# Where ScalarE pads keys and queries, and where VectorE finishes a choice, in a gated-attention and mixture-of-experts kernel

## The chip, the cores and the metric

The kernel runs on one core of a Trainium2 chip. The metric is the device time of one execution in microseconds (us). The engines are named as in the profile: PE is TensorE (PEld its weight loads), DVE is VectorE, ACT is ScalarE, POOL is GpSimd, and SP is the engine that issues most DMAs.

## The reference

```python
def _attn_ref(q, k, v, f_logit):              # all (4, 8, 768, 48)
    f = 1.0 / (1.0 + np.exp(-f_logit))
    for t in range(S):
        state = f[:, :, t, :, None] * state + np.einsum('bhd,bhe->bhde', k[:, :, t], v[:, :, t])
        y[:, :, t] = np.einsum('bhd,bhde->bhe', q[:, :, t], state)
    return y

def _moe_ref(x, w_gate, w1, w2, capacity):    # x (3072, 384), 8 experts, inner width 1024
    logits = x @ w_gate
    expert_idx = np.argmax(logits, axis=1)    # one expert per row, the first of equal ones
    ...                                       # its probability is gate_w
    disp[e, counts[e]] = x[i]                 # rows sorted by expert, up to the capacity
    ...
    h = np.maximum(np.einsum('ecd,edf->ecf', disp, w1), 0.0)
    y = np.einsum('ecf,efd->ecd', h, w2)
    out[i] = gate_w[i] * y[expert_idx[i], pos[i]]
```

The rows `x` of the second part are the attention outputs, all heads of a token side by side.

## The kernel before, in words

The attention half works in 24 chunks of 128 tokens (6 chunks for each of 4 batches), with all 8 heads of a chunk at once. It is written as a loop over slots n = 0 to 24. Each slot works at several chunks: in slot n the keys and queries of chunk n + 3 are padded, those of chunk n + 2 are transposed and scaled, scores of chunk n + 1 are made, the values of chunk n are applied, and the rows of chunk n - 1 are finished. Within this part the order of instructions on every engine is the order in which the code is written; nothing reorders it. The mixture of experts follows and is ordered by a scheduler.

The steps that matter here, with their lines:

- `kq_pad` (L407 on POOL in slots 0 to 6, L409 on ACT from slot 7, `PAD_ACT = 7`): copies a loaded chunk of keys and queries (`ld_kq`, 3 buffers) into a padded tile `kqp` (2 buffers), which `kq_in` of the next slot reads. Behind it `load("kq", n + 6)` issues the two DMAs (L210) that fill the buffer just read.
- `kq_in`: 16 PE transposes (L366) into two `psT` tiles in PSUM, which DVE scales into `kT` and `qT` (L415).
- `keys_pe` / `keys_out`: 8 PE transposes of the keys (L451) into the same `psT` pool of two, copied out by ACT as `kn` (L457).
- `scores_pe` / `scores_out`: 16 products (L426) into two `psA` tiles, copied out by ACT as `AT` (L432), then masked by POOL (L434).
- `update` (L488), then `rank_pe` (L675, L676, L679, L682), `rows_pe` (L543) and `values` (L522) follow on PE in that order. `update` and `rank_pe` write one `psA` tile, the side bank; `rows_pe` writes another; the pool has two.
- `y_out` (L534, `yT`), `rows_copy` (L559, `rows`) and `rows_parts` (L569, `parts`) on ACT. `rows` and `parts` read what `rows_pe` made and free that `psA` tile.
- `sig` (L357, `pf`) in even slots and `split_high` (L135) in slots 9, 11, 17, 20 to 23 stand on ACT as well.
- A choice of experts is made for a group of 3 or 4 chunks: `choose_sum` on POOL, `choose_max` on DVE (L583 to L586) at the end of a slot, and in the next slot `choose_first` (L591 `r_wm`, L593 `tally`) on DVE. This way is used for five groups, so that `choose_first` runs in slots 6, 10, 14, 17 and 20. In the same slot `rank_pe` on PE reads the choice: L675 and L676 read older tiles, L679 and L682 read the new `tally`.

The lines that make the ranking wait for the choice:

```python
    nc.tensor.matmul(pr, onesb, ohc.unsqueeze(1)..., start=(base is None), stop=False)      # L676
    for c in range(nch - 1):
        nc.tensor.matmul(pr[:, c + 1 :], onesb, oh[:, c].unsqueeze(1)..., ...)              # L679
    marks["rank"] = nc.tensor.matmul(pr, tri, oh, start=False, stop=True)                   # L682
```

Of the kernel before, what the change touches and what calls it, by code (L numbers as in the profile page):

```python
# [29 lines left out]
def kernel(  # L30
# [47 lines left out]
    PAD_ACT = 7  # L78
# [116 lines left out]
    def pairs(nm, n, nt):  # L195
        b, t0 = n // CPB, n % CPB * C
        return srcs[nm][b, :, t0 : t0 + nt, :].rearrange("h (t j) d -> t h (j d)", j=2)

    def load(nm, n):
        if n >= (NT // 2 if nm == "f" else NT):  # L200
            return
        t = loads[nm, n % NLOAD[nm]]
        if nm == "v":
            b, t0 = n // CPB, n % CPB * C
            nc.sync.dma_start(t[:, :, :D], srcs[nm][b, :, t0 : t0 + C, :].rearrange("h p d -> p h d"))
            return
        t = t.rearrange("t h j d -> t h (j d)")
        if nm == "kq":
            for h, x in enumerate(nm):
                nc.sync.dma_start(t[64 * h : 64 * h + 64], pairs(x, n, C))  # L210
        elif n == 0:
            for h, queue in enumerate((nc.sync, nc.scalar)):
                hs = slice(4 * h, 4 * h + 4)
                queue.dma_start(t[:64, hs], pairs(nm, 0, C)[:, hs])
        else:
            nc.sync.dma_start(t, pairs(nm, 2 * n, 2 * C))

    def loaded(nm, n):
        return loads[nm, n % NLOAD[nm]]
# [132 lines left out]
    def sig(u):  # L352
        if u >= NT // 2:
            return
        cuts = (0, 64, P) if u == 0 else (0, P)
        for r0, r1 in zip(cuts, cuts[1:]):
            pace["ins"] = nc.scalar.activation(  # L357
                pf[u % 2][r0:r1, :, :, :D], loaded("f", u)[r0:r1].rearrange("t h j d -> t j h d"), AF.Sigmoid
            ).ins
# [43 lines left out]
    def kq_pad(n):  # L403
        if n < NT:
            src = loaded("kq", n).rearrange("t h j d -> t j h d")
            if n - 3 < PAD_ACT:
                nc.gpsimd.tensor_copy(kqp[n % 2][:, :, :, :D], src)  # L407
            else:
                nc.scalar.activation(kqp[n % 2][:, :, :, :D], src, AF.Copy)  # L409

    def kq_in(n):
        pts = transposes(*((psT.tile([P, NP, C], F32, name="psT"), kqp[n % 2], h) for h in range(2)))
        for nm, pt, by, made in (("kT", pts[0], Sufb[n % 2], kTs), ("qT", pts[1], Rqs.pop(n), qTs)):
            t = abuf.tile([P, NP, C], F32, name=nm, bufs=3)
            nc.vector.tensor_tensor(t[:R].rearrange("r p t -> r (p t)"), pt, by[:R], op=ALU.mult)  # L415
            made[n] = t
# [22 lines left out]
    def first(n):  # L439
        return n % CPB == 0  # L440

    def last(n):
        return n % CPB == CPB - 1
# [145 lines left out]
    def choose_first(g, m, w):  # L589
        wm = abuf.tile([P, m], F32, name="r_wm")  # L590
        nc.vector.tensor_reduce(out=wm, in_=w, axis=AX.X, op=ALU.max)  # L591
        oh = tallies[-1][:, 1 : m + 1]
        nc.vector.tensor_tensor(oh, w, wm.unsqueeze(2).broadcast_to([P, m, NE]), op=ALU.is_equal)  # L593
        chosen[g] = oh, m
# [149 lines left out]
    def early_job(n, at):  # L744
        for step, arg in EARLY.get((n, at), ()):
            step(arg)
# [19 lines left out]
    quarters, half = [0] * DT, []  # L766
# [59 lines left out]
    def slot(n):  # L826
        slot_now["n"] = n
        prev, cur, nxt = 0 <= n - 1 < NT, 0 <= n < NT, 0 <= n + 1 < NT
        kqn, fn = 0 <= n + 2 < NT, 0 <= n + 3 < NT
        tail = n - 1 >= NT - NCH  # L830
        keyed = cur and not last(n)
        done = ends.get(n - 1)
        if keyed and n:
            keys_out(n, keys_pe(n))
        if prev and not (cur and first(n)):
            y_out(n - 1)
        if nxt:
            pas = scores_pe(n + 1)
        if 0 < n < PAD_ACT:
            kq_pad(n + 3)  # L840
        if n == 3:
            nc.gpsimd.tensor_copy(ring[:, :, DM + NE : W], tokid[:, :RING].unsqueeze(2))
        while half:
            choose_first(*half.pop())
        for g in full:
            choose_sum(*g)
        if n == 1:
            f_in(4)
        if kqn:
            kq_in(n + 2)  # L850
        if n % 2 and fn and n not in (1, 9, 15):
            f_in(n + 3, n + 4)
        if nxt:
            scores_out(n + 1, pas)
        if n == 0:
            sig(2)
        if prev and cur and first(n):
            y_out(n - 1)
        if n % 2 == 0 and n > 0 and fn:
            sig((n + 4) // 2)  # L860
        if n in PIECE_SPLIT:
            split_high(pieces[PIECE_SPLIT.index(n)])
        loads_of(n)
        early_job(n, 0)
        if cur:
            inter(n)
        if n in (9, 15):
            f_in(n + 3, n + 4)
        early_job(n, 1)
        if keyed:  # L870
            pu = update(n)
        if split_at["n"] == n:
            pc = split_pe()
        ranks = [(g, chosen[g][1], rank(g, None)) for g in list(chosen) if not done or g != done[0]]
        if keyed:
            state(n, pu)
        if split_at["n"] == n:
            split_count(pc)
        ranked = [(g, m, pick(*job)) for g, m, job in ranks]
        if tail:  # L880
            for g, m, job in ranked:
                put(*job)
                queue.extend(range(g, g + m))
            ranked = []
        if keyed:
            carry(n)
        if n == 0:
            kq_pad(3)
            load("kq", 6)
        if nxt:  # L890
            for s in range(SCATTERS.get(n, 2)):
                flush_scatter()
        if fn:
            F = decay(n + 3)
        if prev:
            px = rows_pe(n - 1)
            if tail:
                rows_logits(n - 1, px)
                rows_copy(n - 1, px)
                chosen[n - 1] = choose_one(row_at(n - 1), abuf, tallies[-1][:, 1:2]), 1  # L900
            else:
                rows_copy(n - 1, px)
                rows_parts(n - 1, px)
        if fn and n >= PAD_ACT:
            kq_pad(n + 3)
            load("kq", n + 6)
        if n in QUARTERS:
            k, parts = QUARTERS[n]
            for part in range(parts):
                split_low(pieces[k], nc.gpsimd, PARTS, quarters[k])  # L910
                quarters[k] += 1
        if fn:
            decay_back(n + 3, F)
        for g, m, job in ranked:
            put(*job)
            queue.extend(range(g, g + m))
            if g + m == SPLIT:
                split_at["n"] = n + 1
        while full:
            g = full.pop()  # L920
            half.append((*g, choose_max(*g)))
        if prev and done and not tail:
            g, m = done
            if n - 1 >= NT - 2 * NCH:
                sum_parts(g, m)
                chosen[g] = choose(rows_at(g, m), m, abuf, tallies[-1][:, 1 : m + 1]), m
            else:
                full.append(done)
        if cur:
            values(n)  # L930
        if n % 2 == 0 and n and fn:
            load("f", (n + 4) // 2 + 2)
        if n == 1:
            f_in(5)
        if tail:
            early_job(n, 2)
            g, m = done
            place(*rank(g, psT))
            queue.extend(range(g, g + m))
            flush_scatter()  # L940
        else:
            early_job(n, 2)
        for k in pieces:
            if k >= DT and PIECE_SPLIT[k] == n:
                split_low(pieces[k], nc.vector)
        if n == 4:
            nc.gpsimd.tensor_copy(cap, cap_i[:, 0:1])
        if n == NT - 5:
            ins = nc.sync.dma_start(xg0, dispv[0, : T_FIRST[0]].rearrange("(k p) w -> p k w", p=P))
            tc.declare_no_dep(ins.ins, group="late", reason="later tokens of this expert go to rows of their own")  # L950
            after(ins, early_ins[0], "the rows of the early tokens")
        if n == NT - 3:
            checks.append(check_decay())
        if n == NT - 2:
            pc = psT.tile([P, 1], F32, name="psT")
            nc.tensor.matmul(pc, onesb[:R], checks[0][:R], start=True, stop=True)
            nc.vector.tensor_copy(bad_i, pc)
# [533 lines left out]
```

## Time and profile before

| what | value |
|---|---|
| median of 3 runs | 373.35 us (372.59, 373.35, 375.57) |
| the profiled execution's own time | 375.17 us |
| its span, first to last instruction | 373.4 us |
| PE busy | 362.1 us, 97% of the span |
| DVE busy | 247.8 us, 66% |
| ACT busy | 223.8 us, 60% |
| POOL busy | 166.5 us, 45% |
| slots 7 to 20 (53.4 to 125.4 us of the span) | 72.0 us |
| mean granted clock of TensorE | 0.990 of full speed |

The profile is one execution, seen from its first to its last instruction; 1.8 us of its own time lie outside the span. A busy PE is one that has matmuls under way, not one at its peak. A time in the trace counts from the start of the span, and a number in brackets behind a row is the idle time of that engine before it, with what ended it.

### The profile page before, as it was taken

Reading aid. Unit: us, or ns where it says so; the run is one execution under the profiler, and the core shown is the slowest. Engines: PE = TensorE matmul, PEld = TensorE weight load, DVE = VectorE, ACT = ScalarE, POOL = GpSimd, SP = SyncE. Lnnn points to the kernel's source line nnn. Section 1 sums busy time; section 2 is a strip of 40 time slices with the busy share of each in tenths; the row PEclk is TensorE's granted clock in tenths of the full one; section 3 lists DMA queues with packets and bytes.
Section 4 is the critical chain, followed back from the end, with each engine's and each line's share of the span. In section 5 each row is a group of like instructions: output and inputs, shape, how many; then the busy total and the mean of one; then the engine's idle time right before and its main releaser. Section 6 shows DMA issues by size and latency. Waiting matters only on the chain.

```text
span 373.4 us, 10082 instructions
## 1 busy us (share of the span) xinstructions
PE 362.1 (97%) x3895; PEld 340.8 (91%) x3895; DVE 247.8 (66%) x533; ACT 223.8 (60%) x458; POOL 166.5 (45%) x275
## 2 busy tenths in 40 slices
PE   8999999999899999999999999999999999999993
PEld 7999898888787889999899999999999999999993
DVE  4898988979687866753676296857757665570300
ACT  3356677877586763255477475759578586583310
POOL 6665556675757675235613702127117244144012
PEclk9999999999899999999999999999999999999997
DMA  8999999999997432476696979799797997721001
GB/s 153 187 177 224 205 207 227 256 214 226 213 227 164 130 114 105 133 237 204 191 239 188 286 196 242 212 187 319 169 204 247 172 208 253 129 94 52 14 23 40
DMA packets 111351, 67.86 MB, mean 182 GB/s; under 512 B 93646, under 2 KB 105844, under 8 KB 111296
## 3 DMA queue, kind: packets, MB, share of 16 engines
q1 hardware_dynamic: 107504, 57.09, 69.1%
q0 software_dynamic: 3520, 9.97, 7.7%
q8 instruction: 32, 0.52, 0.6%
q14 instruction: 23, 0.19, 0.2%
q10 hardware_dynamic: 272, 0.10, 0.1%
HBM read 49.46 MB, written 11.43 MB: 163 GB/s over the span
## 4 chain that ended last, share of the span: by engine, by line
PE 84%; issue 8%; ACT 3%; POOL 2%; DVE 1%; POOLq 1%; ACTq 0%
PE psM L1222 15%; PE psA L754 9%; PE psM L1015 9%; PE psT L754 9%; PE psM L754 7%; PE psA L426 6%; PE psY L522 6%; PE psA L543 5%; PE psT L366 4%; PE psY L468 3%; PE psA L488 3%; PE psT L451 3%; PE psF L366 2%; POOL out_dram L326 2%; PE psA L376 2%
## 5 line engine op out<-in xcount | busy, mean ns | idle before, releaser
L326 POOL DMA_INDIRECT out_dram<-yo,g_ti x30 | 31.3, 1042 | 55.6 <-ACT yo L1019 31.7
L434 POOL TENSOR_SCALAR_AFFINE_SELECT AT<-AT 128x512 f32<-128x512 f32 x48 | 29.4, 637 | 23.3 <-ACT AT L432 23.2
L1015 PE MATMUL psM<-w2h,hh 128*128 128x384 f32 (+2 forms) x112 | 37.5, 340 | 0.0
L1015 PE MATMUL psM<-w2l,hh 128*128 128x384 f32 (+2 forms) x112 | 37.3, 338 | 0.0
L1015 PE MATMUL psM<-w2h,hl 128*128 128x384 f32 (+2 forms) x112 | 37.2, 338 | 0.0
L135 ACT ACTIVATE w2h<-raw 128x768 fp32r<-128x768 f32 x32 | 27.0, 844 | 11.2 <-DMA raw<-in_moe_w_dram 11.2
L1222 PE MATMUL psM<-hh,w2h 128*128 128x440 f32 (+3 forms) x96 | 33.7, 351 | 0.0
L1222 PE MATMUL psM<-hh,w2l 128*128 128x440 f32 (+3 forms) x96 | 33.7, 351 | 0.0
L1222 PE MATMUL psM<-hl,w2h 128*128 128x440 f32 (+3 forms) x96 | 33.6, 350 | 0.0
L144 DVE TENSOR_TENSOR w2l<-raw,w2h 128x768 fp32r<-128x768 f32 x28 | 27.8, 994 | 7.7 <-ACT w2h L135 6.9
L386 DVE TENSOR_TENSOR_SCAN Suf<-psF,direv 112x511 f32<-112x511 f32 x24 | 29.1, 1212 | 4.5 <-PE psF L366 4.5
L432 ACT ACTIVATE AT<-psA 128x512 f32<-128x512 f32 x48 | 26.4, 612 | 8.9 <-PE psA L426 5.6
L1242 POOL COPY yo<-yq 128x384 uint16<-128x384 uint16 (+4 forms) x16 | 11.9, 790 | 40.1 <-DMA yq<-yp 38.2
L426 PE MATMUL psA<-qT,kT 48*128 48x128 f32 x384 | 29.4, 293 | 0.0
L400 DVE TENSOR_TENSOR_SCAN Rq<-psF,d 112x512 f32<-112x512 f32 x24 | 29.4, 1223 | 0.0
L326 POOL DMA_INDIRECT disp<-rows,ri x24 | 24.8, 1034 | 9.5 <-issue 4.3
L144 DVE TENSOR_TENSOR w1l<-raw,w1h 128x1024 fp32r<-128x1024 f32 x21 | 26.5, 1269 | 2.9 <-ACT w1h L135 2.6
L761 DVE SCALAR_TENSOR_TENSOR hl<-psA,hh 128x224 fp32r<-128x224 f32 (+8 forms) x26 | 14.2, 547 | 21.3 <-ACT hh L760 19.3
L559 ACT ACTIVATE rows<-psA 128x384 f32<-128x384 f32 x24 | 11.8, 491 | 26.0 <-PE psA L543 19.6
L522 PE MATMUL psY<-AT,ld_v 128*48 128x128 f32 (+1 forms) x384 | 26.9, 278 | 0.0
L426 PEld LDWEIGHTS psA<-qT,kT 48*128 48x128 f32 x384 | 25.8, 201 | 0.5 <-issue 0.5
L135 ACT ACTIVATE w1h<-raw 128x1024 fp32r<-128x1024 f32 x24 | 24.8, 1060 | 1.9 <-DMA raw<-in_moe_w_dram 1.9
(253 smaller groups left out, 1041.7 us busy)
## 6 DMA issues: line engine op xcount, KB each, us to landing
raw<-in_moe_w_dram SPq DMA_DIRECT2D x24, 512.0 KB
raw<-in_moe_w_dram SPq DMA_DIRECT2D x32, 384.0 KB
ld_kq<-in_k_dram SPq DMA_DIRECT2D x24, 192.0 KB
ld_kq<-in_q_dram SPq DMA_DIRECT2D x24, 192.0 KB
ld_v<-in_v_dram SPq DMA_DIRECT2D x24, 192.0 KB
ld_f<-in_f_logit_dram SPq DMA_DIRECT2D x11, 384.0 KB
xg<-disp SPq DMA_DIRECT2D x6, 589.5 KB
xg<-disp SPq DMA_DIRECT2D x3, 393.0 KB
```

What stands on the lines that cost most here:

```text
L135: return nc.scalar.activation(hi, raw, AF.Copy)
L144: engine.tensor_tensor(lo[cs], raw[cs], hi[cs].bitcast(F32), op=ALU.subtract)
L326: ins = nc.gpsimd.indirect_dma_start(out=dst, out_offset=bass.IndirectOffsetOnAxis(ap=idx, axis=0), in_=rows, in_offset=None, bounds_check ...
L386: nc.vector.tensor_tensor_scan(out=_view(Suf[:R], m - 1, [[-1, m]]), data0=_view(F, m, [[-1, m]]), data1=_view(direv[:R], m - 1, [[-1, m]] ...
L400: nc.vector.tensor_tensor_scan(out=Rq[:R], data0=F, data1=d1[:R], initial=0.0, op0=ALU.mult, op1=ALU.max)
L426: nc.tensor.matmul(pas[s][:, p], kTs[n][r, p], qTs[n][r, p], start=True, stop=True)
L432: nc.scalar.activation(AT[:, s], pas[s], AF.Copy)
L434: nc.gpsimd.affine_select(AT[:, s], AT[:, s], pattern=[[0, NP], [1, C]], compare_op=ALU.is_ge, fill=0.0, base=0, channel_multiplier=-1)
L522: nc.tensor.matmul(py[b][64 * g : 64 * g + m, a, :], vt[:, 2 * p + s, :m], AT[:, s, p, :], start=(first(n) and a == 0), stop=(a == NP // 2 ...
L754: nc.tensor.matmul(ph[:, :T], a[:, c, fs], x[:, c, :T], start=(n == 0), stop=(n == 3 * DT - 1))
L1015: nc.tensor.matmul(py[:n], x[:, ks], a[:, ft], start=(ft == 0 and m == 0), stop=(ft == FT - 1 and m == 2))
L1222: nc.tensor.matmul(pys[c][:, :T], a[:, ft, cs], x[:, :T], start=(ft == 0 and n == 0), stop=(ft == FT - 1 and n == 2))
```

## The change

Two steps of `slot` are moved, and nothing is added or removed. `kq_pad(n + 3)` with its loads, for slots 7 to 20, moves from behind `rows_copy` and `rows_parts` to a place ahead of `split_high`, of the slot's other loads and of the row copies. `choose_first` moves from ahead of `kq_in(n + 2)` to behind it.

```diff
@@ -840,14 +840,14 @@
-        while half:
-            choose_first(*half.pop())
         for g in full:
             choose_sum(*g)
         if n == 1:
             f_in(4)
         if kqn:
             kq_in(n + 2)
+        while half:
+            choose_first(*half.pop())
         if n % 2 and fn and n not in (1, 9, 15):
             f_in(n + 3, n + 4)
@@ -858,6 +858,9 @@
         if n % 2 == 0 and n > 0 and fn:
             sig((n + 4) // 2)
+        if fn and n >= PAD_ACT:
+            kq_pad(n + 3)
+            load("kq", n + 6)
         if n in PIECE_SPLIT:
             split_high(pieces[PIECE_SPLIT.index(n)])
         loads_of(n)
@@ -901,9 +904,6 @@
                 rows_copy(n - 1, px)
                 rows_parts(n - 1, px)
-        if fn and n >= PAD_ACT:
-            kq_pad(n + 3)
-            load("kq", n + 6)
         if n in QUARTERS:
```

On DVE, in a slot with a choice (here the second of the five, slot 10), the two scalings `kT` and `qT` stood behind `r_wm` and `tally`; `-` is before, `+` is after.

```order
 L585 TENSOR_TENSOR r_w<-rows,r_m 128x32
 L586 TENSOR_TENSOR r_w<-r_w,desc 128x32
+L415 TENSOR_TENSOR kT<-psT,Suf_141 112x512
+L415 TENSOR_TENSOR qT<-psT,Rq 112x512
 L591 TENSOR_REDUCE r_wm<-r_w 128x4
 L593 TENSOR_TENSOR tally<-r_w,r_wm 128x32
-L415 TENSOR_TENSOR kT<-psT,Suf_141 112x512
-L415 TENSOR_TENSOR qT<-psT,Rq 112x512
 L502 TENSOR_TENSOR U<-psA,S_147 112x192
 L642 TENSOR_TENSOR r_sel<-psA,tally 128x4x8
```

The choice now stands between the scalings and `U`; PE's rows are the same in both kernels, L679 with its wait for DVE behind L488, L675 and L676.

On ACT, at the first of the fourteen moved pads (slot 7, which pads chunk 10):

```order
 L534 ACTIVATE yT<-psY 112x2x128 x2
 L432 ACTIVATE AT<-psA 128x512 x2
-L559 ACTIVATE rows<-psA 128x384
-L569 ACTIVATE parts<-psA 128x32
 L409 ACTIVATE kqp_122<-ld_kq_104 128x16x48
+L559 ACTIVATE rows<-psA 128x384
+L569 ACTIVATE parts<-psA 128x32
 L457 ACTIVATE kn<-psT 128x4x64
 L457 ACTIVATE kn<-psT 128x4x48
```

The pad stood between `parts` and the next slot's `kn`, and stands now between `AT` and `rows`.

On SP, the loads of the same two slots (7 and 8). Before:

```order
L205 DMA ld_v_114<-in_v_dram 128x8x48
L210 DMA ld_kq_104<-in_k_dram 64x8x96
L210 DMA ld_kq_104<-in_q_dram 64x8x96
L205 DMA ld_v_116<-in_v_dram 128x8x48
L122 DMA raw<-in_moe_w_dram 128x1024
L210 DMA ld_kq_105<-in_k_dram 64x8x96
L210 DMA ld_kq_105<-in_q_dram 64x8x96
```

After:

```order
L210 DMA ld_kq_104<-in_k_dram 64x8x96
L210 DMA ld_kq_104<-in_q_dram 64x8x96
L205 DMA ld_v_114<-in_v_dram 128x8x48
L210 DMA ld_kq_105<-in_k_dram 64x8x96
L210 DMA ld_kq_105<-in_q_dram 64x8x96
L205 DMA ld_v_116<-in_v_dram 128x8x48
L122 DMA raw<-in_moe_w_dram 128x1024
```

The loads of keys and queries go out ahead of the slot's values and of the expert weights (`raw`).

## Rows read from the trace of the kernel before

**Rows 1.** The page, part 1: busy us (share of the span) xinstructions.

```profile
PE 362.1 (97%) x3895; PEld 340.8 (91%) x3895; DVE 247.8 (66%) x533; ACT 223.8 (60%) x458; POOL 166.5 (45%) x275
```

**Rows 2.** Busy time by stretch: us, busy by engine (instructions), granted clock, DMA share, GB/s.

```profile
53.40:125.40 72.00, 68.89 (x1416) 60.23 (x1414) 60.00 (x128) 53.08 (x127) 46.90 (x79) 0.98 1.03 215
...
150.00:332.00 182.00, 182.00 (x1007) 176.30 (x1006) 119.39 (x245) 118.36 (x209) 62.96 (x66) 1.00 0.80 208
```

**Rows 3.** Waits of PE from 53.4 to 125.4: total us, times, longest.

```profile
PE psY L468 <- issue: 1.0, 2, 0.7
PE psA L488 <- ACT AT L432: 0.7, 3, 0.3
PE psT L366 <- ACT kn L457: 0.6, 3, 0.2
PE psT L366 <- issue: 0.6, 1, 0.6
```

**Rows 4.** Timeline of slot 10 (a choice): start us, us, engine, line [idle before].

```profile
66.22 0.18 DVE L591 TENSOR_REDUCE r_wm<-r_w 128x4 f32<-128x32 f32 x1
...
66.44 0.19 DVE L593 TENSOR_TENSOR tally<-r_w,r_wm 128x32 bf16<-128x32 f32 x1
...
66.57 0.69 DVE L415 TENSOR_TENSOR kT<-psT,Suf 112x512 f32<-112x512 f32 x1
...
67.18 0.68 DVE L415 TENSOR_TENSOR qT<-psT,Rq 112x512 f32<-112x512 f32 x1
...
67.77 0.22 PE L679 MATMUL psA<-tally,onesb 128*128 128x24 bf16 x3
...
68.13 0.36 DVE L502 TENSOR_TENSOR U<-psA,S 112x192 f32<-112x192 f32 x1 [0.27 <-PE psA L682]
```

**Rows 5.** Timeline of slots 6 and 17, two more choices.

```profile
46.65 0.68 DVE L415 TENSOR_TENSOR qT<-psT,Rq 112x512 f32<-112x512 f32 x1
...
46.96 0.22 PE L679 MATMUL psA<-tally,onesb 128*128 128x24 bf16 x3
...
105.79 0.68 DVE L415 TENSOR_TENSOR qT<-psT,Rq 112x512 f32<-112x512 f32 x1
...
106.19 0.19 PE L679 MATMUL psA<-tally,onesb 128*128 128x16 bf16 x2
```

**Rows 6.** The pad: its group in the list by line, then timelines around it.

```profile
L409 ACT ACTIVATE kqp<-ld_kq 128x768 f32<-128x768 f32 x14 | 11.9, 847 | 0.0
...
29.98 0.46 PE L451 MATMUL psT<-ident,kT 64*128 64x64 f32 x8
...
30.54 0.60 ACT L457 ACTIVATE kn<-psT 128x256 f32<-128x256 f32 x2 [0.73 <-PE psT L451]
...
74.92 1.79 SPq L210 DMA_DIRECT2D ld_kq<-in_q_dram  x1
...
77.17 0.87 ACT L357 ACTIVATE pf<-ld_f 128x768 f32<-128x768 f32 x1
...
78.16 0.49 ACT L559 ACTIVATE rows<-psA 128x384 f32<-128x384 f32 x1
...
79.20 1.12 PE L426 MATMUL psA<-qT,kT 48*128 48x128 f32 x16
...
83.54 0.49 ACT L559 ACTIVATE rows<-psA 128x384 f32<-128x384 f32 x1 [1.61 <-PE psA L543]
...
84.01 0.85 ACT L409 ACTIVATE kqp<-ld_kq 128x768 f32<-128x768 f32 x1
...
84.30 0.46 PE L451 MATMUL psT<-ident,kT 64*128 64x64 f32 x8
...
85.48 0.61 ACT L457 ACTIVATE kn<-psT 128x256 f32<-128x256 f32 x2 [0.63 <-PE psT L451]
```

**Rows 7.** Busy time by stretch, columns as in rows 2, around the lower clock.

```profile
99.00:100.00 1.00, 0.60 (x13) 0.43 (x12) 0.36 (x1) 0.63 (x1) 1.00 (x3) 0.96 1.20 288
100.00:101.00 1.00, 1.00 (x22) 1.00 (x20) 0.25 (x1) 0.00 (x0) 0.30 (x1) 0.50 1.15 263
```

## The prediction

> **What bounds the kernel now.** I read the page's first part, then the stretch that the change touches, then what PE waits for there. PE is busy for 97% of the span; no other engine passes 66% [rows 1]. The moved steps lie in slots 6 to 20. From 53.4 to 125.4 us PE is busy for 68.89 of 72.00 us, and from 150 to 332 us, in the mixture of experts, for all 182 [rows 2]. So a microsecond that PE gains or loses in the slots arrives at the end: nothing behind them has room to absorb it. The reader is to take two limits from this. No edit here can give back more than the 3.1 us that PE is idle in the stretch, and most of these do not hang on the moved steps: 1.6 us are "issue", 0.7 us wait for `AT` and 0.6 us for `kn` [rows 3]. A wait newly put in front of PE costs its full length.
>
> **The choice behind the scalings.** This half moves two short DVE instructions in five slots. In slot 10, `r_wm` starts at 66.22, `tally` 0.22 us later and lasts 0.19 us, so the choice is known at 66.63. PE's L679, which reads it, starts at 67.77 without waiting: the choice is 1.14 us early [rows 4]. What it delays is `kT`, which starts at 66.57. But `kT` cannot start before PE's transposes are out, and in four of the five slots DVE had nothing to wait for but those, or came free at the same moment; nobody waits for `kT` and `qT` before the next slot, since scores are made one slot after the scaling. So the gain from earlier scalings is zero, and what hides their cost today is a whole slot of distance.
>
> After the change the choice begins when `qT` lets DVE go. From `kT` to `qT` it takes 0.61 us from start to start [rows 4], so I let `r_wm` start 0.61 us behind `qT`, `tally` 0.22 us behind that, and end after 0.19 us (0.18 us where the group has three chunks): 1.02 us behind the start of `qT`. That start itself stays, because PE sets it.
>
> - Slot 10: 67.18 + 1.02 = 68.20, against L679 at 67.77: 0.43 us late.
> - Slot 6, the first chunk of a batch, has no L468 in PE's row, so L679 comes sooner: 46.65 + 1.02 = 47.67 against 46.96: 0.71 us [rows 5].
> - Slot 17, the last chunk of a batch, has no `update`: 105.79 + 1.01 = 106.80 against 106.19: 0.61 us [rows 5].
> - Slots 14 and 20 repeat slot 10 within 0.02 us: 0.43 us each.
>
> The sum is 2.6 us. A hand-over from one engine to the next comes on top. The trace has none from DVE to L679, since that matmul never waited. The nearest row is `kn` at 30.54, 0.10 us after the L451 it waited for was out at 29.98 + 0.46 [rows 6]; five of these make 0.5 us. That gives 2.6 to 3.1 us, and I take 2.9, nearer the upper end because every wait in these slots shows some hand-over. Queued behind L679 on PE are L682, L543 and L522, and behind the choice on DVE are `U`, which waits for L682 in any case [rows 4], and the two scans of the slot. So PE and DVE slip by about the same amount, `rows` on ACT slips with L543, and the next slot begins that much later. I see nothing that gives the time back.
>
> **The pads ahead of the row copies.** This half moves fourteen ACT instructions of 847 ns, which today never wait (idle before them 0.0 us in all) [rows 6]. Ahead of `rows` ACT is often idle, because `rows` waits for L543: 1.61 us in slot 13 [rows 6]. There the pad fits in without moving `rows`. Where `pf` stands in front and the slot is short, it does not: in slot 12 `pf` ends at 78.04 and `rows` starts at 78.16. A pad between them starts at about 77.95, 0.1 us of overlap as between the neighbours here, so `rows` starts 0.75 us after that, at about 78.7, and with its 0.49 and the 0.19 us of `parts`, less the overlaps, the `psA` tile is free at about 79.3. The scores that take it start at 79.20 and use the second tile with their second matmul: 0.1 us late. Slot 18 is the same case; the other twelve have idle time in front of `rows`, or the scores come late enough. I set the cost at 0.1 to 0.2 us.
>
> What could be gained is at the pad's old place, in front of `kn`. Without a pad, in slot 3, `kn` starts 0.56 us after L451 (29.98 to 30.54). With a pad it is often the same, but in six slots it is late; in slot 14 it starts at 85.48, 1.18 us after L451 and 0.63 us after the pad has ended [rows 6]. ACT was idle in these 0.63 us, so the pad is not what it waited for, and its earlier end buys nothing. At most PE gets back all that it waits for `kn`, 0.6 us, and all its "issue" stalls, 1.6 us, which lie in the same region: 2.2 us [rows 3]. I take zero, since the row nearest to it shows idle time and not a pad. The Trainium skill speaks for this: by "Perfetto Trace Analysis", section "Tensor Engine Instruction (MATMUL, LD_WEIGHTS)", the end of a matmul in a profile is estimated and not observed, so L451 may have been out later than its row says. No run so far shows it.
>
> Each pad carries its loads with it. They stand now ahead of the slot's `v` and `raw` loads on SP. The pads never waited for data, and the nearest case has room: the second load of chunk 16 is issued by 76.71 (74.92 + 1.79), and its pad in slot 13 moves from 84.01 to the end of `AT` at 81.93 (83.54 - 1.61), which leaves 5.2 us [rows 6]. The loads issue earlier too, as their buffers come free earlier. `v` slips by two issues of at most 1.8 us each [rows 6] and is used three slots later. `split_high` slips by one pad in slots 9, 11, 17 and 20; its readers are DVE and POOL, which have slack. I cost these at nothing; if data were late, ACT would hold `rows` and `kn` back behind the pad.
>
> **Sum.** +2.9 us for the choice, +0.1 for the pads: +3.0 us, 0.8%. On the profiled execution that is 375.17 + 3.0 = 378.2 us. That execution lies 1.8 us above the median of the runs, and I give the time against the median: 373.35 + 3.0 = 376.3 us.
>
> **The rivals.**
>
> *The pads free `kn`, and the lower clock goes with it (faster).* If the late `kn` does come from the pad in front of it, 2.2 us come back. One of the six lies in slot 16, where PE then stalls (0.60 busy from 99 to 100) and the clock falls to 0.50 for three rows of a microsecond and 0.83 in a fourth [rows 7], about 1.7 us lost. Were that to go as well, the sum is 3.0 - 2.2 - 1.7 = -0.9 us: 372.4 us. For it speaks that no slot without a pad shows a late `kn`; against it, six slots with a pad do not either, and ACT's idle time. It decides in the trace at `kn` 0.56 us behind L451 in all slots. Without the clock it gives 374.1 us. Chances 0.07 and 0.11.
>
> *The new stalls let the clock fall (slower).* PE would now stop for 0.5 to 0.8 us in five slots. The one fall in the slots followed stalls of this kind: PE 0.60 busy, then 0.50 of full speed, the 1.2 GHz level [rows 7]. Each further fall at 1.7 us gives 378.0 us, two 379.7. Against it: PE had another stall of 0.6 us, in front of L366 [rows 3], and the stretch's mean clock of 0.98 leaves room for no second fall (1.7 of 72.0 us is 0.024) [rows 2]. By the Trainium skill, "TensorE: Matmul & The Clock Gate", section "A second HAM failure mode: psum-queue depth-cycling", short idle times between groups of matmuls can be enough to make the clock swing; the trace bears it out once, and once does not. Chance 0.20.
>
> *The choice's wait costs nothing.* If something else held PE at that point, as a mask that L522 needs, the stall would be time lost anyway, and the whole change about 373.4 us. The waits of PE name no L522 and no L543 [rows 3], so I give it 0.08.
>
> **How the numbers follow.** The forecast, 375.4 to 377.3 us, gets the rest, 0.54. The range 373.0 to 379.0 us leaves out the faster rival whole, two falls of the clock, and a part of the cases at either edge, together about 0.2. The runs of before lie 0.8% apart, so about 1%, 3.7 us, is what can be told from no change: faster means under 369.6, slower over 377.1 us. No rival reaches the first; 0.05 is for what I have not seen. Slower takes most of the clock's rival and the upper edge of the forecast, where 3.1 us and a little from ACT meet: 0.25. Within 1% is left with 0.70.
>
> **What would show it.** In the profile after, L679 should have a new wait of 0.4 to 0.8 us for DVE's `tally` in slots 6, 10, 14, 17 and 20, about 2.9 us together; `kT` should start at L366's end as before; ACT should be idle before `rows` for some 0.75 us less, and more before `kn`; `kn` should still be late in slots of the same region. I am wrong if L679 does not wait (then the order has more room than I found), if the late `kn` vanish, or if the slots after a choice shrink by what the choice lost.

## The result, and the profile after

The changed kernel takes 378.30 us (median of 12 runs, 376.41 to 381.97) against 374.07 us for the kernel before in the same comparison (12 runs, 372.55 to 375.78): a ratio of 1.0121, 95% interval 1.0089 to 1.0152. Ratios and their intervals are here and below over the fast runs alone, those less than 1.5% above the fastest of the same kernel, and medians over all runs. The forecast was 3.0 us and the comparison gave 4.5 (3.3 to 5.7). The profiled execution took 377.96 us, with a span of 376.3 us.

First the page's part 1 of the changed kernel, to set beside [rows 1], and its busy time by stretch, to set beside [rows 2] (the same slots, moved by about 1 us, and the mixture of experts).

```profile
PE 356.7 (95%) x3895; PEld 334.7 (89%) x3895; DVE 247.9 (66%) x533; ACT 224.5 (60%) x458; POOL 168.8 (45%) x275
```

```profile
54.40:126.10 71.70, 67.29 (x1416) 58.84 (x1414) 60.19 (x128) 52.36 (x126) 46.96 (x79) 1.00 1.05 217
150.00:332.00 182.00, 181.04 (x1001) 175.05 (x1000) 118.31 (x244) 117.68 (x206) 64.71 (x65) 1.00 0.80 208
```

PE is now idle for 4.4 us in the slots where it was idle for 3.1, and for 1.0 us in the mixture of experts, where it never was. The granted clock stayed at 1.00, without the fall of [rows 7]. What PE waits for, from 20 to 155 us (us in total, times, longest), to set beside [rows 3]:

```profile
PE psA L679 <- DVE tally L593: 2.6, 5, 0.7
PE psA L426 <- ACT parts L569: 1.4, 1, 1.4
PE psA L488 <- ACT AT L432: 0.8, 3, 0.3
PE psA L488 <- DMA ld_v<-in_v_dram: 0.6, 1, 0.6
PE psT L366 <- issue: 0.5, 1, 0.5
PE psT L366 <- ACT kn L457: 0.4, 2, 0.3
```

The first row is the forecast's new wait. In the timeline its five instances stand in slots 6, 10, 14, 17 and 20:

```profile
47.96 0.22 PE L679 MATMUL psA<-tally,onesb 128*128 128x24 bf16 x3 [0.58 <-DVE tally L593]
69.56 0.22 PE L679 MATMUL psA<-tally,onesb 128*128 128x24 bf16 x3 [0.33 <-DVE tally L593]
90.07 0.22 PE L679 MATMUL psA<-tally,onesb 128*128 128x24 bf16 x3 [0.39 <-DVE tally L593]
106.22 0.19 PE L679 MATMUL psA<-tally,onesb 128*128 128x16 bf16 x2 [0.73 <-DVE tally L593]
123.58 0.19 PE L679 MATMUL psA<-tally,onesb 128*128 128x16 bf16 x2 [0.52 <-DVE tally L593]
```

The forecast for these was 0.71, 0.43, 0.43, 0.61 and 0.43 us before hand-overs, so single slots came out up to 0.13 us off it, either way. DVE's side of slot 10, to set beside [rows 4]:

```profile
67.83 0.69 DVE L415 TENSOR_TENSOR kT<-psT,Suf 112x512 f32<-112x512 f32 x1 [0.36 <-PE psT L366]
68.43 0.68 DVE L415 TENSOR_TENSOR qT<-psT,Rq 112x512 f32<-112x512 f32 x1
69.03 0.17 DVE L591 TENSOR_REDUCE r_wm<-r_w 128x4 f32<-128x32 f32 x1
69.24 0.26 DVE L593 TENSOR_TENSOR tally<-r_w,r_wm 128x32 bf16<-128x32 f32 x1
69.92 0.36 DVE L502 TENSOR_TENSOR U<-psA,S 112x192 f32<-112x192 f32 x1 [0.41 <-PE psA L682]
```

`r_wm` starts 0.60 us behind `qT` and `tally` 0.21 us behind that, as worked out (0.61 and 0.22). `kT` now waits for L366: there was nothing to gain by starting it earlier. `tally` ends at 69.50 and L679 starts at 69.56, so the hand-over is 0.06 us. On ACT, three groups of the list by line (instructions | busy, mean ns | idle before, releasers), the first to set beside [rows 6], and then the last two of them in the kernel before:

```profile
L409 ACT ACTIVATE kqp<-ld_kq 128x768 f32<-128x768 f32 x14 | 12.2, 871 | 0.0
L559 ACT ACTIVATE rows<-psA 128x384 f32<-128x384 f32 x24 | 11.9, 496 | 19.1 <-PE psA L543 13.7 <-DVE rows L601 2.8 <-issue 2.5
L457 ACT ACTIVATE kn<-psT 128x256 f32<-128x256 f32 (+1 forms) x38 | 11.8, 355 | 15.1 <-PE psT L451 12.2 <-PE psA L426 1.3 <-ACT parts L569 0.7
```

```profile
L559 ACT ACTIVATE rows<-psA 128x384 f32<-128x384 f32 x24 | 11.8, 491 | 26.0 <-PE psA L543 19.6 <-DVE rows L601 5.9
L457 ACT ACTIVATE kn<-psT 128x256 f32<-128x256 f32 (+1 forms) x38 | 11.6, 355 | 8.8 <-PE psT L451 7.6 <-PE psA L426 1.0
```

The pads filled ACT's idle time ahead of `rows`, which in the kernel before was 26.0 us and is 19.1 now, and the time came back ahead of `kn`, 8.8 us before and 15.1 now. That is what the prediction said the pads would do, at two thirds of its size: 6.9 us for fourteen pads are 0.49 us each, and it had some 0.75.

### The profile page after: what moved, and what is told of

Read it like the earlier page. It is cut to its first block, busy times and chain, and to the rows that moved or that the text cites. A ratio compares the mean times of both kernels' runs of the same rounds, so it can differ in the third digit from the quotient of the medians.

```text
span 376.3 us, 10082 instructions
## 1 busy us (share of the span) xinstructions
PE 356.7 (95%) x3895; PEld 334.7 (89%) x3895; DVE 247.9 (66%) x533; ACT 224.5 (60%) x458; POOL 168.8 (45%) x275
## 4 chain that ended last, share of the span: by engine, by line
PE 74%; issue 9%; DMA 5%; DVE 4%; POOL 2%; ACT 2%; SPq 2%; POOLq 1%; ACTq 0%; DVEq 0%
PE psM L1222 14%; PE psA L754 9%; PE psM L1015 9%; PE psT L754 9%; PE psM L754 7%; PE psA L543 4%; PE psY L522 4%; PE psA L426 4%; PE psT L366 3%; PE psY L468 2%; DMA ld_v<-in_v_dram 2%; PE psT L451 2%; DMA ld_f<-in_f_logit_dram 2%; PE psA L488 2%; POOL out_dram L326 2%
## 5 line engine op out<-in xcount | busy, mean ns | idle before, releaser
L434 POOL TENSOR_SCALAR_AFFINE_SELECT AT<-AT 128x512 f32<-128x512 f32 x48 | 29.6, 640 | 19.4 <-ACT AT L432 19.1
L1242 POOL COPY yo<-yq 128x384 uint16<-128x384 uint16 (+4 forms) x16 | 13.3, 875 | 38.3 <-DMA yq<-yp 36.7
L426 PE MATMUL psA<-qT,kT 48*128 48x128 f32 x384 | 28.0, 281 | 1.9 <-ACT parts L569 1.4
L426 PEld LDWEIGHTS psA<-qT,kT 48*128 48x128 f32 x384 | 24.4, 189 | 2.7 <-ACT parts L569 1.6
L522 PE MATMUL psY<-AT,ld_v 128*48 128x128 f32 (+1 forms) x384 | 26.0, 272 | 0.0
L415 DVE TENSOR_TENSOR kT<-psT,Suf 112x512 f32<-112x512 f32 x24 | 16.5, 688 | 10.4 <-PE psT L366 10.1
```

Source lines behind the costliest of these rows:

```text
L426: nc.tensor.matmul(pas[s][:, p], kTs[n][r, p], qTs[n][r, p], start=True, stop=True)
L434: nc.gpsimd.affine_select(AT[:, s], AT[:, s], pattern=[[0, NP], [1, C]], compare_op=ALU.is_ge, fill=0.0, base=0, channel_multiplier=-1)
L522: nc.tensor.matmul(py[b][64 * g : 64 * g + m, a, :], vt[:, 2 * p + s, :m], AT[:, s, p, :], start=(first(n) and a == 0), stop=(a == NP // 2 ...
```

## The experiments

They ran in three series, each against the kernel before on the same chip; the first two series ran on one chip and the third on another. The kernel's own medians were 374.91 us (26 runs, 373.65 to 376.88), 373.17 (23 runs, 369.90 to 377.62) and 372.68 (35 runs, 368.77 to 376.70). "P" in the table stands for pads moved (with their loads unless it is said), "C" for the choice moved. The two lengths come from each kernel's one profile, and move with chance events that are told below (e9 and e10 also have L718 in the second length and not in the first): from PE's first L522 in slot 5 to that in slot 21, which holds all five choices, and from there to the end of the span.

| kernel | ratio to before (95%) | waits at L679, us | slot 5 to 21 | slot 21 to end |
|---|---|---|---|---|
| before, first profile | 1 | 0 | 85.55 | 244.65 |
| after (P, C) | 1.0121 (1.0089 to 1.0152) | 2.6 | 85.97 | 246.85 |
| e1 C | 1.0111 (1.0072 to 1.0150) | 2.5 | 86.88 | 245.35 |
| e2 P | 1.0045 (1.0018 to 1.0072) | 0 | 83.53 | 245.31 |
| e3 P, C between kT and qT | 1.0046 (1.0022 to 1.0069) | 0.2 | 84.03 | 245.88 |
| e4 P, C, ranking behind L543 | 1.0059 (1.0033 to 1.0084) | 0 | 85.44 | 244.92 |
| e5 before again | one run, 378.61 us | 0 | 85.77 | 247.57 |
| e6 after again (P, C) | 1.0000 (0.9965 to 1.0035) | 2.2 | 82.14 | 243.91 |
| e7 P without loads | 1.0042 (0.9999 to 1.0085) | 0 | 80.34 | 248.03 |
| e8 C, qT scaled twice | 1.0129 (1.0071 to 1.0187) | 5.5 | 92.64 | 244.09 |
| e9 before, L718 later | 1.0027 (0.9989 to 1.0064) | 0 | 79.45 | 248.68 |
| e10 after, L718 later (P, C) | 1.0045 (1.0006 to 1.0083) | 3.1 | 82.13 | 249.40 |
| e11 C again | 0.9998 (0.9957 to 1.0038) | 2.5 | 82.78 | 245.36 |
| e12 P again | 1.0019 (0.9978 to 1.0060) | 0 | 82.25 | 243.87 |

### First series: the parts, and the wait taken away

**e1, the choice alone.**

```diff
-        while half:
-            choose_first(*half.pop())
...
         if kqn:
             kq_in(n + 2)
+        while half:
+            choose_first(*half.pop())
```

> Of the change only the choice is moved (r_wm and tally behind kT and qT); the pads and the loads stand as before. Theory A, my forecast's terms, with the pads nearly free: five waits of PE's L679 for tally, 2.6 us together in the profile, and 2.6 to 3.1 us more than the kernel before; the rest of what the whole change costs (4.2 to 4.5 us) then appears here neither. Theory B, the pads or their loads cost the rest: also 2.6 to 3.1 us here, and 1.2 to 1.6 us with the pads alone. Theory C, the choice costs all of it, its waits and something behind them (the hand-over to the mixture of experts, or a lower clock after the stalls): 4.2 to 4.5 us here.

378.75 us, 3.8 us by medians and 4.2 by the ratio. The five waits are there with 2.5 us. So the choice alone cost more than its waits, as theory C has it, although the interval (2.7 to 5.6 us) also holds 2.9.

**e2, the pads alone.**

```diff
+        if fn and n >= PAD_ACT:
+            kq_pad(n + 3)
+            load("kq", n + 6)
         if n in PIECE_SPLIT:
...
-        if fn and n >= PAD_ACT:
-            kq_pad(n + 3)
-            load("kq", n + 6)
```

> Of the change only the fourteen pads on ScalarE and their loads are moved; the choice stands as before. Theory A: 0.1 to 0.2 us more than before, no wait at L679, kn still late in some slots of the same region. Theory B: 1.2 to 1.6 us more, with a new wait that can be named (rows or kn later on ScalarE, or values that come late on SP). Theory C: 0.0 to 0.2 us. A rival of the prediction, that the pads free kn and the clock's fall goes: 0.6 to 3.9 us less than before, and no late kn.

376.79 us, by the ratio 1.7 us over (0.7 to 2.7): theory B. But the trace has no wait in slots 7 to 20 that names it, and slot 5 to 21 is 2 us shorter than in the first profile of before, which holds the clock's fall of [rows 7] (1.7 us). What this execution lost, it lost where the two kernels have the same instructions in the same order: 3.0 us by slot 3 (a wait of 1.5 us and a fall of the clock, below), and 1.0 us at the hand-over to the mixture of experts (below).

**e3, the choice between the scalings.**

```diff
         made[n] = t
+        if nm == "kT":
+            while half:
+                choose_first(*half.pop())
```

> The changed kernel, but the choice stands between kT and qT and so ends one scaling, 0.61 us, sooner. The five waits of 0.33 to 0.7 us at L679 should fall to 0.1 us in slots 6 and 17 and to nothing in the others, 0.1 to 0.2 us in all. Theories A and C (all costs hang on the waits): 0.1 to 0.4 us over the kernel before. Theory B (the pads cost the rest whatever the choice does): 1.2 to 1.8 us over it.

**e4, the ranking behind the row products.**

```diff
-        ranks = [(g, chosen[g][1], rank(g, None)) for g in ...]
...
             px = rows_pe(n - 1)
+            ranked = [... pick(*job) for ... rank(g, None) ...]
```

> The changed kernel, but in slots 6, 10, 14, 17 and 20 PE ranks (L675 to L682) behind the row products L543 and not ahead of them; the choice stays behind the scalings. L543 with its 0.8 us then lies between the last product of the update and L679, so that a tally that is 0.3 to 0.7 us late for L679 is in time. No wait at L679 then. Theories A and C: 0.1 to 0.4 us over the kernel before; theory B: 1.2 to 1.8 us over it. If the stall only moves (L682 then holds U, r_sel or L522 up) the time stays at that of the changed kernel, 4.2 to 4.5 us over.

The waits went as expected: one of 0.2 us (slot 17) is left in e3, none in e4. The row of e3 (its L682 is L679 of the others):

```profile
PE psA L682 <- DVE tally L596: 0.2, 1, 0.2
```

The times are 1.7 and 2.2 us over the kernel before. Against the changed kernel's 4.5 us (from the comparison ahead of this series), taking the waits away gave back 2.3 to 2.8 us, about the 2.6 us that they measured. By these times, of two comparisons, the waits were worth about their length, and some 1.7 us were left, which fits theory B. The profiles say it less plainly: from slot 5 to 21, e3 is 1.9 us shorter than the changed kernel, but e4 only 0.5, with 1.1 us of waits for `kn` and 0.8 us of "issue" at L468 in the place of L679's.

### Second series: the same kernels once more, the loads, and a larger dose

**e5, the kernel before again (no edit).**

> The kernel before, profiled once more, to see what one profiled execution may differ by where nothing is changed. If the fall of the clock in slot 16 and the hand-over to the mixture of experts without a stall (both in the first profile of before, neither in the changed kernel nor with the choice or the pads alone) belong to the kernel, they are here again: slot 16 about 2.3 us longer than in the changed kernel, and no wait of 1.0 us at L754. If they are chance, one of them is gone, or the clock falls in another place, as at 31 us with the pads alone.

Both were chance. Slot 16 has no stall and no fall of the clock here (from 99 to 101 us PE is busy throughout, clock 1.00). Instead PE waits 3.9 us in slot 21 for the gather of the early tokens' rows, and the clock falls during the wait and stays low for 3 us and more behind it. The execution took 378.61 us, longer than any of the 23 timed in this series (up to 377.62), so the length of this wait is no measure of the usual one. The wait, and three stretches around it:

```profile
126.50 0.69 PE L718 MATMUL psF<-ident,xg 128*128 128x128 f32 x2 [3.88 <-DMA xg<-disp]
```

```profile
124.00:125.00 1.00, 0.00 (x0) 0.00 (x0) 0.54 (x1) 0.00 (x0) 0.42 (x1) 0.89 1.08 175
125.00:128.00 3.00, 1.50 (x19) 1.17 (x21) 0.36 (x1) 0.38 (x1) 0.00 (x0) 0.50 0.35 124
128.00:131.00 3.00, 3.00 (x35) 2.93 (x32) 1.07 (x5) 0.58 (x2) 1.70 (x3) 0.50 0.00 0
```

The first execution of the same kernel did not wait there. The late `kn` of [rows 6] are gone as well, with the pads at their old place. Slot 14 of this execution:

```profile
85.37 0.85 ACT L409 ACTIVATE kqp<-ld_kq 128x768 f32<-128x768 f32 x1
85.66 0.46 PE L451 MATMUL psT<-ident,kT 64*128 64x64 f32 x8
86.22 0.60 ACT L457 ACTIVATE kn<-psT 128x256 f32<-128x256 f32 x2
```

`kn` starts 0.56 us behind L451, and not 1.18. Late `kn` stood in the profiles of before, after and e1 to e4, in up to seven slots from slot 9 on. In the second and third series, from slot 9 on, there was one that came 0.3 us or more too late, in slot 13, in e5 and in e9, and none in the other six.

**e6, the changed kernel again (no edit).**

> The changed kernel once more, profiled and timed in the same rounds as the next two. Its five waits at L679 should be there again, 2.5 to 2.7 us. If the 1.4 us wait of L426 for parts at 30 us, the 1.0 us wait at L754 and the longer end belong to the change, they are here again; if they are chance, at least one is not. Time: 4.0 to 5.0 us over the kernel before by either theory.

373.25 us against 373.17: no difference (by the ratio 1.3 us under to 1.3 over), with 2.2 us of waits at L679 in four slots (in slot 10 PE waited 0.5 us for `v` ahead of L488 instead). In slot 12 `v` was late once more, by the row of L488 and the semaphore row ahead of it:

```profile
78.22 0.58 PE L488 MATMUL psA<-ld_v,kn 128*64 128x48 f32 x15 [1.34 <-ACT yT L534]
L488 PEldq EVENT_SEMAPHORE  x1: 51/51/51, 78.1 to 78.1; - x1
```

The profile names `yT`, which ended at the same moment. But in after L488 of this slot started at 78.47, 0.04 us behind the start of its `yT` (78.43), so it does not wait for that; and there, too, such a semaphore row, at 78.4 us, ended the 0.6 us that the profile puts down to `v`. So this execution waited some 4 us in the slots, for the choice and for `v`, and the total shows nothing of it. The waits at 165 us and the long end of the first profile were chance; the time of 4.0 to 5.0 us over was wrong by either theory.

**e7, the pads without their loads.**

```diff
+        if fn and n >= PAD_ACT:
+            kq_pad(n + 3)
         if n in PIECE_SPLIT:
...
         if fn and n >= PAD_ACT:
-            kq_pad(n + 3)
             load("kq", n + 6)
```

> Only the fourteen pads on ScalarE are moved; their loads of keys and queries stay at their old place, behind the slot's values and the expert weights on SP, and the choice stays where it was. If the order of the loads costs what the pads alone cost (1.7 us in the last runs, of which my forecast had 0.1), this kernel is 0.0 to 0.3 us over the kernel before. If the place of the pads on ScalarE costs it, it is 1.2 to 2.0 us over. By my forecast both are 0.1 to 0.2.

1.6 us over, but with an interval of 0.0 to 3.2 it tells nothing apart.

**e8, a larger dose.**

```diff
             made[n] = t
+            if nm == "qT" and half:
+                nc.vector.tensor_tensor(t[:R]..., pt, by[:R], op=ALU.mult)
```

> Only the choice is moved, and in its five slots qT is scaled twice ahead of it (0.61 us more each, from start to start; the second writes the same values again). Each wait at L679 should grow by 0.6 us: 5.5 to 5.6 us in all in place of 2.5. If a microsecond of this wait costs a microsecond, the kernel is 5.6 to 6.1 us over the kernel before. If the choice alone really cost the 4.2 us that it measured, with 2.5 us of waits (1.7 us for each), the time is 8 to 9.5 us over.

6.1 us by medians, 4.8 by the ratio, and 5.5 us of waits in four slots (the fifth was covered by another wait). One for one fits, and the interval (2.7 to 7.0 us by the ratio) does not allow the 8 to 9.5. But one for one is not shown: all six executions had a mean granted clock of 0.981 to 0.993, so their time holds falls of the clock beside the waits, and in the same series 2.2 us of such waits cost nothing that could be measured (e6). In the profiled execution, which at 381.42 us was the longest of its runs, the clock fell three times in the slots: with the waits of 1.61 and 1.64 us in slots 6 and 17, and behind a stall of 2.30 us at L366 in slot 8, which has no choice. The first of them:

```profile
48.46 0.22 PE L681 MATMUL psA<-tally,onesb 128*128 128x24 bf16 x3 [1.61 <-DVE tally L595]
```

```profile
46.00:48.00 2.00, 0.81 (x18) 0.68 (x19) 1.93 (x5) 1.75 (x4) 1.04 (x2) 1.00 1.00 198
48.00:51.00 3.00, 2.54 (x30) 2.50 (x31) 2.60 (x7) 0.58 (x2) 1.46 (x3) 0.51 1.13 205
```

### Third series: where the time could be given back

**e9 and e10, the first readers of the gather later, in the kernel before and in the changed one.**

```diff
-        (NT - 3, 1): ((early_prep, 0),),
-        (NT - 3, 2): ((early_prep, 1), (early_prep, 2)),
+        (NT - 3, 2): ((early_prep, 0), (early_prep, 1), (early_prep, 2)),
```

> The kernel before, but PE's first two transposes of the gathered rows (L718 of part 0), the first instructions that need the gather, stand at the end of slot 21, behind L522, and not ahead of its update: some 2.6 us later in PE's row. Theory D, why the changed kernel cost nothing in the second series: where the slots run without late kn, PE of the kernel before comes to L718 before the gather has landed (3.9 us of waiting in its second profile, with the clock low for 6.8 us behind it), and a choice's stall ahead of it only shortens that wait. By D, where the slots run so, this kernel is 1 to 3 us below the kernel before, and where kn is late it is level with it, within 0.5 us. If the wait at L718 does not bear on the time, it is level in both cases.

> The changed kernel with the same move of L718. By theory D it is 2.5 to 3.5 us over the kernel before with that move (the run ahead of this one), whichever way the slots run, since the wait that could swallow the five stalls at L679 is gone or short; against the unmoved kernel before it is then 0 to 2 us over without late kn, and 3 to 4.5 us over with it. If the stalls are swallowed elsewhere, it is level with the run ahead of this one.

Theory D falls in the form it had. e9 is 1.0 us over the kernel before (0.4 under to 2.4 over) and not 1 to 3 below; the move may have a price of its own, since L718 now waits 1.1 us for `x0l`. e10 lies 1.5 us over e9 by medians and 0.7 by the ratios, with intervals that overlap, and not 2.5 to 3.5. Yet from slot 5 to 21 the two profiles differ by 82.13 - 79.45 = 2.7 us.

**e11 and e12, the choice alone and the pads alone once more (the edits of e1 and e2).**

> Only the choice is moved, as in the first run of the first series, once more. With late kn in the profile: 2.6 to 4.2 us over the kernel before, as there. Without: by theory D 0 to 2 us over, with 2.5 to 3.1 us of waits at L679 all the same. If the choice costs the same whichever way the slots run, 2.6 to 4.2 us.

> Only the pads and their loads are moved, once more. If the 1.7 us that they cost in the first series belong to the edit, 1 to 2 us over the kernel before; if they belong to the place where a load happened to land in that series, within 0.5 us of it. My forecast had 0.1 to 0.2.

The choice alone: 0.9998 (1.6 us under to 1.4 over; 0.9 over by medians), with the same 2.5 us of waits:

```profile
PE psA L679 <- DVE tally L593: 2.5, 5, 0.7
```

The pads alone: 0.7 us over, 0.8 under to 2.2 over. The choice does not repeat the 4.2 us of the first series; the pads' interval holds their 1.7 us as well as nothing. Since this series ran on another chip, the chip is a rival for the difference between e1 and e11; it is none for that between e1 and e6, which ran on one.

## Where the time behind the slots goes either way

Besides the gather of e5, the traces show three places where one execution loses 1 to 3 us and another nothing. None of them is at a moved step.

*The start.* L426 waits 1.0 to 1.6 us at about 30 us in after, e2, e3, e5, e10 and e12, and 0.7 us or less in the others. In after, the chain behind it:

```profile
29.14 0.84 ACT L357 ACTIVATE pf<-ld_f 128x768 f32<-128x768 f32 x1 [2.70 <-DMA ld_f<-in_f_logit_dram]
30.26 0.19 ACT L569 ACTIVATE parts<-psA 128x32 f32<-128x32 f32 x1
30.50 1.04 PE L426 MATMUL psA<-qT,kT 48*128 48x128 f32 x13 [1.36 <-ACT parts L569]
```

ACT holds `rows` and `parts` back behind a load of `f`. In e2, e3 and e12 slot 3 comes 2.4 to 3.0 us later than in the first profile of before, in the others within 0.4 us of it. The wait is about half of that. The rest is the clock, which fell behind it in these three (waits of 1.5 to 1.6 us) and not in after, e5 and e10 (1.0 to 1.4 us). In e2, the wait and the stretch behind it:

```profile
31.70 0.71 PE L426 MATMUL psA<-qT,kT 48*128 48x128 f32 x8 [1.51 <-ACT parts L569]
33.00:36.00 3.00, 3.00 (x60) 2.54 (x54) 1.29 (x2) 0.83 (x2) 0.68 (x1) 0.54 1.34 189
```

*The hand-over to the mixture of experts.* In after, e1, e2 and e3, L754 waits 1.0 us at about 165 us for `hl`, and in no other profile. The row of after:

```profile
165.07 0.37 PE L754 MATMUL psA<-x0h,w1h 128*128 128x224 f32 x1 [0.96 <-DVE hl L761]
```

*The second gather.* In e5, e7, e9 and e10, L754 waits 1.6 to 2.2 us at 184 to 191 us. e7 has the wait and e6 has not; rows of POOL, DVE and SP in e6, then in e7:

```profile
174.97 0.94 POOL L326 DMA_INDIRECT out_dram<-yo,g_ti  x1 [0.30 <-DVE xl L1194]
175.03 0.19 DVE L987 TENSOR_TENSOR g_d<-xg,g_m 128x32 f32<-128x32 f32 x1
175.36 0.38 SPq L1144 DMA_DIRECT2D xg<-disp  x1
175.91 1.88 POOL L144 TENSOR_TENSOR w2l<-raw,w2h 128x768 fp32r<-128x768 f32 x1
```

```profile
174.99 0.94 POOL L326 DMA_INDIRECT out_dram<-yo,g_ti  x1 [0.30 <-issue]
175.35 2.52 DVE L988 TENSOR_TENSOR g_d<-xg,g_m 128x32 f32<-128x32 f32 x1
175.93 1.88 POOL L144 TENSOR_TENSOR w2l<-raw,w2h 128x768 fp32r<-128x768 f32 x1
178.00 0.38 SPq L1145 DMA_DIRECT2D xg<-disp  x1
183.63 0.19 DVE L986 TENSOR_REDUCE g_m<-xg 128x4 f32<-128x32 f32 x1 [4.13 <-DMA xg<-disp]
184.63 0.49 PE L754 MATMUL psA<-xh,w1h 128*128 128x480 f32 x1 [2.19 <-DVE hl L761]
```

In e7 `g_d` starts 0.3 us later against POOL's rows, and takes 2.52 us in place of 0.19: it ends when POOL's `w2l` does (175.93 + 1.88 = 177.81, against 177.87). SP's gather, which may overwrite `xg` only when `g_d` has read it, goes out 2.6 us later, DVE waits 4.13 us for it at `g_m`, and `hl`, queued behind `g_m`, holds PE up. The Trainium skill, "SBUF — State Buffer", section "Who interferes with whom", says that a DVE instruction with two inputs in SBUF contends with a GpSimd instruction that reads SBUF, over ports that one of them holds alone; the two ends, 0.06 us apart, agree with it. The page also lets the order of issue decide who is blocked; that does not fit `g_d`, which had started 0.58 us ahead of `w2l` and was held all the same. In e9 and e10 `g_d` took 2.51 us in the same way, and in e5 the row ahead of it, `g_ti`, took 1.36 us. In the ten profiles in which L754 does not wait there, `w2l` held the later `g_sp` (seven, 1.7 to 2.4 us) or neither. Behind the wait the clock fell in e7, to 0.54 from 185 to 188 us.

So a shift of some tenths of a microsecond can cost or save 2 us and more here. In the second and third series the kernels without a choice's waits had this loss in three of four profiles (e5, e7, e9; not e12), those with them in one of four (e10; not e6, e8, e11). That is the direction in which 2.5 us of waits could come to nothing in the total. With one profile for each kernel it is argued and not shown.

The timed executions carry a mean granted clock each, and it bears on this. In the first series 24 of the 26 executions of the kernel before had 0.995 or more, in the second 9 of 23 and in the third 18 of 35, against 8 of 12 in e6 and 9 of 12 in e11. Among the executions with 0.995 or more, the mean of e6 lies 1.2 us over that of the kernel before and the mean of e11 1.4 us over, not 0.0 and -0.1. So part of what the changed order costs does not show in these totals, because more of the executions of the kernel before had a lower clock. The split was made afterwards and its groups are small and unequal. By it e7 and e12, without a choice's waits, come out 1.3 and 1.2 us over as well, so it does not price the waits.

## Why the prediction was right, and where not

- *L679 waits in five slots, 2.6 to 3.1 us:* right, 2.6 us in the changed kernel and 2.2 to 3.1 us in e1, e6, e10 and e11. The hand-over was taken at 0.10 us and measured 0.05 to 0.06, and the lateness ahead of it summed to 2.3 us in place of 2.6, so the 2.9 taken was 0.3 too much. `tally`, taken at 0.19 us, lasted 0.18 to 0.39 us in these profiles and 0.8 in slot 6 of e10, where the wait was 1.19 us. That the waits come from the choice is shown by e3 and e4, which take them away, and by e8, which doubles them.
- *Earlier scalings gain nothing:* right; no profile has PE wait for `kT` or `qT` in these slots. That `kT` waits for L366 holds in all five slots of the first profile after, in e6, e10 and e11 only in slot 6.
- *The pads cost 0.1 to 0.2 us and gain nothing:* no wait in slots 7 to 20 shows them to cost more, and ACT's idle time moved as said, by 0.49 us a pad. The total says 1.7 us (0.7 to 2.7) in e2 and 0.7 (0.8 under to 2.2 over) in e12. Whether something of this belongs to the edit stays open.
- *The loads cost nothing:* not quite. `v`, which now goes out behind the keys and queries, was late for L488 in slot 12 of after (0.6 us) and in slots 10 and 12 of e6 (0.5 and 1.3 us), and in no profile with the loads in their old order. The prediction gave it room because it is used three slots later in the code; in the trace, the `v` of slot 12 was issued at 67.6 us for a use at 76.3 in the kernel before, and at 70.5 us for a use at about 77 in e6, where the loads of `v` of this stretch took 6.2 to 8.4 us from issue to landing. This cost, put at nothing, is a term that the sum lacked, though not in every execution: e2, e10 and e12 have the new order and no such wait.
- *The late `kn` do not come from the pads:* right. They stayed in the profile after, and went in e5, where the pads had not moved. What makes L451's end late in some series was not found. The rival that the pads free `kn` falls.
- *The new waits let the clock fall:* not at their size; waits of 0.3 to 1.2 us in after, e1, e6, e10 and e11 were followed by no fall in the slots. At 1.61 and 1.64 us it happened (e8). The length of the wait does not settle it: the fall of [rows 7] came behind 0.7 us, and L754's wait of 2.1 us in e5 had none behind it.
- *"A microsecond that PE gains or loses in the slots arrives at the end: nothing behind them has room to absorb it":* this step failed. One profile showed PE busy for all of 150 to 332 us [rows 2], and I took that for a property of the kernel. Other executions of the kernel before, and of its variants, wait 1 to 4 us behind the moved steps, at transfers and at a DVE instruction held up by POOL. The total went up by more than the 2.5 us of waits in the first comparisons (+4.5, +4.2) and not measurably in later ones (0.0 in e6, 1.3 under to 1.3 over; -0.1 in e11, 1.6 under to 1.4 over). That the waits behind the slots are what took the 2.5 us up is argued; the cause stays open.
- *The total, +3.0 us:* +4.5 us in the comparison that counts (3.3 to 5.7), so 3.0 was too little. The time, 378.30 us, is inside the range of 373.0 to 379.0, above the forecast's 375.4 to 377.3, and over the 377.1 that counted as slower, which had a chance of 0.25. Of the 2.0 us over 376.3, the kernel before, 0.7 us slower in this comparison than in its first three runs, makes 0.7. The first term is confirmed as a wait in front of PE, not as time at the end; of the 1.5 to 1.9 us on top, the late `v` can be 0.6 at most, and the profile after shows no other new wait in the slots. That the total came out on the side and near the size forecast was in part luck: the same edit gave 0.0 us in e6. The profiled pair shows how little one pair tells: 377.96 - 375.17 = 2.8 us looks like the forecast, but of the difference in span 0.3 us lies ahead of slot 5, 0.4 us from slot 5 to 21 (before had a fall of the clock there and after had none) and 2.2 us behind, of which 1.0 at L754.

The best that the runs found is the order of the kernel before: no variant was faster than it.

## What to carry to other kernels

A wait that a reordering puts in front of an in-order queue can be worked out from start times to about 0.2 us, slot by slot (one wait, of 1.19 us in e10, fell outside). Whether it reaches the end is another question: look behind the place, in more than one execution of the unchanged kernel, for waits on transfers and for engines that hold each other up, since these can give back or add as much as the edit costs. Where a kernel's own runs spread by 1 to 2%, repeat the comparison in a second series, and compare the granted clocks of the executions, before a difference of 1% is given a cause.

## What was not expected of the hardware

- One DVE instruction of 128x32 elements took 0.19 us or 2.52 us, by whether it started 0.06 or 0.36 us behind POOL's DMA issue that stood ahead of `w2l` (e6, e7); the other profiles fit, with 0.19 us at 0.20 to 0.26 us behind it (e8, e11, e12) and 2.51 us at 0.36 to 0.37 (e9, e10).
- The kernel before and the changed one had `kn` late by up to 1.0 us in four to six slots from slot 9 on in their first profiles, and in one slot and none in their second. The chip is not the reason: e1 to e4, which had it late, and e5 to e8 ran on one.
- The gather that L718 needs was in time in the first profile of before and 3.9 us late in the second, an execution of 378.61 us, longer than any of the 23 timed ones of that kernel in the series.
